# Moving eight key copies, two V casts and one normalisation within the fixed queues of a fused attention + MLP kernel

## The chip, the cores and the metric

The kernel runs on one core of a Trainium2 chip. A core has a matmul engine (TensorE, "PE" in the profile, with its weight loads shown as "PEld"), a vector engine (VectorE, "DVE"), an activation engine (ScalarE, "ACT"), GpSimd ("POOL") and a DMA-issuing engine (SyncE, "SP"). Each engine works through its own queue of instructions; engines wait for one another through semaphores. The metric is the device time of one execution in microseconds (us), the median of several runs. The profile is of one such execution; its span, 257.8 us, is a little shorter than the device time.

## The reference

Attention over 4 batches, 8 heads, 768 positions and head size 64, in which each query attends only to the 6 best of 24 key chunks of 32 positions (ranked by an upper bound on the score, causally masked), followed by an MLP with softplus.

```python
k_min, k_max = min / max of k over each chunk of 32 positions
ub     = sum over d of max(q*k_min, q*k_max)         # one bound per query and chunk
top    = the 6 chunks with the largest ub (causal)
scores = q @ k.T / sqrt(64), masked to the chosen chunks and to the causal triangle
attn   = exp(scores) / sum(exp(scores))
x      = attn @ v                                    # [3072 tokens, 512]
h      = x @ w_in                                    # [3072, 2048]
out    = softplus(h) @ w_out                         # [3072, 512]
```

## The kernel before

The 3072 tokens are cut into 12 blocks of 256 queries (batch b, block blk of three in the batch). Each block goes through the same steps. `prep`: transposed keys, their chunk minima and maxima, transposed queries, bounds, selection of chunks. `attend`: for each of 4 pairs of heads, scores, exponentials, product with V, normalisation, transposition to x. Then the MLP. The first three blocks (0, 1, 2, all of batch 0) are the ramp: they use TensorE transposes, and TensorE runs filler matmuls on zeros where it has nothing else to do, up to about 23 us. The nine others use DMA transposes, and their attention is mixed with the MLP of earlier blocks.

All instructions are made by small tasks. A scheduler in Python, which models durations, puts them in a fixed order on each engine; at the end, single tasks can be moved by hand. An entry (name, k, to, j) takes the k-th task called `name` that is still found in the order and puts it directly behind the j-th task called `to`. The last figure of a name is the block.

```python
for name, k, to, j in MOVES:
    t = [x for x in order if x.name == name][k]
    order.remove(t)
    order.insert(order.index([x for x in order if x.name == to][j]) + 1, t)
```

The parts of the ramp that matter here, with cuts marked. First the keys. Blocks 0 and 1 write their transposed keys whole into `ka_1`, a buffer that batch 1 needs later, and eight tasks `kcp` copy them to their places in `ka_0` and `kb_0`, which only block 2's scores read:

```python
# kT: PE transposes k -> ps;   kx: DVE, two tensor_reduce (max, min) per half of the heads
kr = add("DVE", 1.26, lambda: (red(0), red(1)), ..., name=f"kx{n}")            # L544
if split:                                          # blocks 0 and 1
    add("ACT", 0.5, kae, ..., name=f"ka{n}")                                   # L552: ka_1 <- ps
    for which, rs in (("ka", slice(0, 64)), ("kb", slice(64, 128))):
        add("DVE", 0.24, lambda: DV.tensor_copy(
            T(which, i)[rs, p2, ks_], T("ka", 1)[rs, p2, ks_]), ..., name=f"kcp{n}")   # L556
    continue
add("ACT", 1.06, lambda: (kab("ka", ...), kab("kb", ...)), ..., name=f"ka{n}")  # L541, block 2: ka_0, kb_0 <- ps
...
# kb0 (L371): DVE memset of 32 x 1536 words in kb_i;  ohka0, ohkb0 (L374): DVE copies of the one-hot rows
add("POOL", 0.6, lambda: PO.dma_start(*oh(which, i, blks)), ..., name="oh" + which)   # L377, for batch 1's ka_1, kb_1
```

Then the queries, the selection and V:

```python
# qT: PE transposes q -> ps;  qb: ACT evacuates it (L609);  qp, qn: DVE, positive and negative parts (L624)
# ub: PE, bounds from qp, qn and the chunk extremes (L646, L647)
# uba: DVE adds the causal mask (L653);  max: DVE MAX8 (L662);  lt: DVE, chunks below the sixth (L672, L675)
# mT: PE transposes the selection (L691);  ma: DVE or ACT evacuates it into qa (L696)
# vc: POOL or ACT casts V to bf16 (L721)
```

And a pair of heads in `attend`:

```python
# s:  PE scores (L749 keys, L756 selection; L775 from block 2 on);  ex: ACT exp (L785);  cm: POOL triangle (L791)
# av: PE product with V (L802)
add("DVE", 0.1, rc, ..., name=f"rc{n}")       # L811 reciprocal of the row sums, in ps
add("DVE", 0.34, nm, ..., name=f"nm{n}")      # L823 osb <- ps * st
add("PE", 0.12, tr, ..., name=f"oT{n}")       # L831 transposes osb -> ps
add("DVE", 0.22, xe, ..., name=f"xe{n}", alt=("ACT", ...))   # L836 x <- ps
# MLP: h: PE (L859), e and g: ACT exp and ln (L865, L869), y: PE (L885), yo: DVE (L890)
```

Of the kernel before, what the change touches and what calls it, by code (L numbers as in the profile page):

```python
# [54 lines left out]
HOLDS = [("q", 1, 1), ("q", 2, 1), ("q", 2, 1)]  # L55

READS = [("q", 1, 0), ("k", 2, 1)]
MOVES = [("holdp", 0, "vc0", 1), ("ldw_in", 0, "holdp", 0), ("ohka", 0, "vc2", 1), ("ohkb", 0, "ohka", 0)]
SHIFT = (0, 0, 8)


# [21 lines left out]
class Graph:  # L83
# [40 lines left out]
    def schedule(self):  # L124
# [157 lines left out]
        assert len(order) == len(self.tasks) + len(self.fills), (len(order), len(self.tasks))  # L282
        for name, k, to, j in MOVES:
            t = [x for x in order if x.name == name][k]
# [737 lines left out]
```

## Time and profile before

| | |
|---|---|
| device time, median of 3 | 259.45 us (259.43 to 259.63) |
| span of the profile | 257.8 us |
| DVE busy | 151.3 us (59%) |
| ACT busy | 199.1 us (77%) |
| POOL busy | 82.8 us (32%) |
| the eight copies, L556 | 285 to 514 ns each |
| memset of `kb`, L371 | 2 times 1338 ns |
| reductions kx of the ramp, L544 | 12 times, 681 ns each (median) |
| V casts on ACT, L721 | 0.65 us each at 15.97 and 16.97 us |

How to read it. The page lists each engine's busy time, the span in slices, and a chain of work followed back from the last instruction. A timeline line is "start, duration, engine, source line, operation, output <- input, count", and a bracket at its end gives how long the engine sat idle before it, and for whom it waited. A waits line is "engine line waited for: us in total, times, longest". A windows line gives the busy time of each engine in a stretch. A matmul's end is modelled, and consecutive matmuls overlap, so for TensorE the starts are what can be compared.

### The profile page before, as it was taken

The page shows a single profiled execution, that of the slowest core. Times are in us where ns is not written, and L with a number is a line of the kernel's source. Part 1 is how long each engine was busy: PE and PEld are TensorE (multiplying, and loading weights), DVE is VectorE, ACT ScalarE, POOL GpSimd, SP SyncE. Part 2 cuts the span into 40 slices and gives each one's busy share as a digit, 9 for nine tenths or more (in the row PEclk, how much of TensorE's full clock was granted, in tenths as well). Part 3 has the DMA queues.
Part 4 walks back from the last instruction along what each step waited for, and adds up shares of the span by engine and source line. Part 5 has one row for each costly group of instructions (what it writes and reads, how often), then busy time and mean ns, then how long its engine had stood idle before and what let it go on. Part 6 is the DMA issues. An engine that isn't in the chain of part 4 may idle for free.

```text
span 257.8 us, 6836 instructions
## 1 busy us (share of the span) xinstructions
PE 251.4 (98%) x2620; PEld 189.5 (73%) x2620; DVE 151.3 (59%) x555; ACT 199.1 (77%) x359; POOL 82.8 (32%) x176
## 2 busy tenths in 40 slices
PE   8999899999999999999999999999999999999994
PEld 6887696687685786878677778677677687686763
DVE  5897958459876983949797138586487310221101
ACT  2677989988494999899389979759689679796570
POOL 3352460356063460458223344323513001010000
PEclk9999999999999999999999999999999999999999
DMA  7999899999986979899963599654992310111202
GB/s 178 269 183 212 202 154 195 232 198 268 170 220 147 220 185 187 208 188 263 164 163 80 128 228 256 138 127 101 227 180 40 101 43 1 43 41 41 84 0 83
DMA packets 119897, 39.64 MB, mean 154 GB/s; under 512 B 113496, under 2 KB 115800, under 8 KB 119864
## 3 DMA queue, kind: packets, MB, share of 16 engines
q1 hardware_dynamic: 114456, 34.09, 60.5%
q0 software_dynamic: 3296, 4.59, 10.4%
q10 hardware_dynamic: 2112, 0.52, 0.9%
q8 instruction: 20, 0.33, 0.5%
q14 instruction: 13, 0.11, 0.1%
HBM read 27.26 MB, written 6.29 MB: 130 GB/s over the span
## 4 chain that ended last, share of the span: by engine, by line
PE 92%; DVE 6%; issue 1%; ACT 0%; DVEq 0%
PE ps L885 32%; PE ps L859 31%; PE ps L775 12%; PE ps L802 7%; PE ps L387 5%; PE ps L537 1%; PE ps L605 1%; DVE kx L571 1%; PE ps L647 1%; DVE qpn L624 1%; PE ps L831 1%; PE ps L646 1%; DVE yo L890 1%; DVE ka L556 1%; PE ps L749 1%; DVE kb L371 1%
## 5 line engine op out<-in xcount | busy, mean ns | idle before, releaser
L859 PE MATMUL ps<-x,w_in_sb 128*128 128x256 bf16 x768 | 100.9, 272 | 0.0
L785 ACT ACTIVATE pt<-ps 128x512 bf16<-128x512 f32 (+1 forms) x192 | 92.0, 562 | 7.8 <-PE ps L775 5.3
L885 PE MATMUL ps<-w_out_sb,g 128*128 128x512 bf16 (+1 forms) x400 | 97.2, 370 | 0.0
L859 PEld LDWEIGHTS <-w_in_sb 128*128 128x128 bf16 x768 | 72.0, 98 | 15.5 <-issue 0.7
L791 POOL TENSOR_SCALAR_AFFINE_SELECT pt<-pt 128x256 bf16<-128x256 bf16 x96 | 40.9, 433 | 126.7 <-ACT pt L785 126.6
L865 ACT ACTIVATE e<-ps 128x512 f32<-128x512 f32 x96 | 57.8, 617 | 30.3 <-PE ps L859 29.1
L885 PEld LDWEIGHTS <-g 128*128 128x128 bf16 x400 | 37.1, 98 | 25.0 <-ACT g L869 0.3
L869 ACT ACTIVATE g<-e 128x1024 bf16<-128x1024 f32 x48 | 51.5, 1072 | 1.0
L890 DVE COPY yo<-ps 128x512 f32<-128x512 f32 (+1 forms) x25 | 16.7, 667 | 44.2 <-PE ps L885 39.9
L811 DVE RECIPROCAL st<-ps 128x4 f32<-128x4 f32 x48 | 8.5, 178 | 36.9 <-PE ps L802 36.4
L802 PEld LDWEIGHTS <-pt 128*128 128x128 bf16 x672 | 26.5, 97 | 3.6
L802 PE MATMUL ps<-v,pt 128*128 128x65 bf16 x672 | 28.0, 193 | 0.0
L775 PE MATMUL ps<-qab,kb 128*128 128x256 bf16 (+1 forms) x168 | 25.8, 259 | 0.0
L775 PE MATMUL ps<-qab,ka 96*128 96x256 bf16 (+1 forms) x168 | 24.6, 259 | 0.0
L457 POOL CAST w<-w 128x512 bf16<-128x512 f32 x36 | 22.1, 628 | 5.2 <-DMA w<-in_q_dram 2.9
L571 DVE TENSOR_REDUCE kx<-w 128x32 bf16<-128x1024 bf16 x18 | 21.3, 1211 | 0.4 <-DMA w<-w 0.2
L775 PEld LDWEIGHTS <-ka 96*128 96x128 bf16 x168 | 15.4, 97 | 6.2 <-DVE qab L696 0.2
L775 PEld LDWEIGHTS <-kb 128*128 128x128 bf16 x168 | 14.7, 97 | 4.8
L387 PE MATMUL ps<-zero 128*128 128x256 bf16 x96 | 15.2, 294 | 1.1 <-DVE zero L355 1.1
L823 DVE TENSOR_TENSOR w<-ps,st 128x256 bf16<-128x256 f32 x36 | 15.2, 422 | 1.1
L662 DVE MAX8 ub<-ub 128x8 f32<-128x24 f32 (+2 forms) x160 | 14.2, 160 | 0.1
L455 POOL CAST v<-w 128x512 bf16<-128x512 f32 x18 | 11.0, 613 | 6.7 <-DMA w<-in_v_dram 6.7
(70 smaller groups left out, 181.9 us busy)
## 6 DMA issues: line engine op xcount, KB each, us to landing
w<-in_v_dram SPq DMA_DIRECT2D x24, 256.0 KB, 4.2
out_dram<-yo SPq DMA_DIRECT2D x23, 256.0 KB, 3.7
w<-in_k_dram SPq DMA_DIRECT2D x22, 256.0 KB, 4.0
w<-in_q_dram SPq DMA_DIRECT2D x22, 256.0 KB, 4.2
w_in_sb<-in_moe_w_in_dram POOLq DMA_DIRECT2D x2, 1024.0 KB, 11.6
w_out_sb<-in_moe_w_out_dram POOLq DMA_DIRECT2D x4, 512.0 KB, 8.9
w<-in_k_dram SPq DMA_DIRECT2D x2, 128.0 KB, 3.0
w<-in_k_dram ACTq DMA_DIRECT2D x2, 128.0 KB, 3.1
```

What stands on the lines that cost most here:

```text
L387: PE.matmul(T(Fill)[:, 0:256], T("zero")[:, 0:128], T("zero"), start=True, stop=True)
L457: PO.tensor_copy(T(b_)[:, :, t], T(xf).rearrange("s (p c) -> s p c", p=NP))
L571: DV.tensor_reduce(T(kx)[:, m].rearrange("d p (t c) -> d p t c", t=NT), T(kt).rearrange("d (p t) (c s) -> d p t c s", t=NT, s=CH), axis=AX ...
L775: PE.matmul(T(sp)[:, z * QB:z * QB + QB - q0], kk[r0:r1, p, (j + z) * 128:(j + z + 1) * 128], qq[r0:r1, p, q0:QB], start=True, stop=True)
L785: AC.activation(T(pt)[:, j:j + 2].rearrange("k j c -> k (j c)")[:, 0:w], T(sp)[:, 0:w], ACT.Exp, scale=SCALE)
L791: PO.affine_select(out=diag, in_=diag, compare_op=ALU.is_ge, fill=0.0, base=0, channel_multiplier=-1, pattern=[[0, 2], [1, 128]])
L802: PE.matmul(o[:, u, h], T(pts[h])[:, j, c0:c0 + 128], T("v", i)[:, j, 2 * p + h, :], start=(j == 0), stop=(j == t0 + u))
L859: PE.matmul(o, T("w_in")[:, dt, ft * 128:(ft + 1) * 128], T(x)[:, dt], start=(dt == 0), stop=(dt == KDM - 1))
L865: AC.activation(T(e)[:, f2 * 2:f2 * 2 + 2].rearrange("f a s -> f (a s)"), T(hp), ACT.Exp)
L869: AC.activation(T(gb)[:, f4 * 4:(f4 + 1) * 4], T(e), ACT.Ln, bias=1.0)
L885: PE.matmul(T(y)[:, 0:w], T(gb)[:, f, u * 128:(u + 1) * 128], T("w_out")[:, f, cs], start=(f == 0), stop=(f == KFF - 1))
L890: add("DVE", 0.06 + 0.54 / parts, lambda y=y, yo=yo, w=w: DV.tensor_copy(T(yo)[:, 0:w], T(y)[:, 0:w]), pr, r=[y], w=[yo], name=f"yo{n}")
```

## The change

The entries added to MOVES do three things.

- Key copies: all eight `kcp`, and batch 1's `kb0` memset ahead of them, go behind the last `xe1` on VectorE, that is behind the last piece of block 1's x. They stood between the one-hot copies and block 1's first normalisation; the memset stood a little behind that.
- V casts: the two ScalarE casts of block 1's V stood one between and one behind the evacuations of block 1's two query halves. Now both stand behind the second.
- Selection: block 1's second pair of `qp`, `qn` goes directly behind the first pair. The reciprocal and normalisation of block 0's last pair of heads (`rc0`, `nm0`, number 3), which stood ahead of the second half of block 1's selection, go behind it, and that pair's transposition (`oT0`) and evacuation (`xe0`) go back with them. The transposition and evacuation of the pair before it (number 2) move a few places too.

The aim is that work which something waits for does not stand behind work that nobody needs yet.

```diff
-MOVES = [("holdp", 0, "vc0", 1), ("ldw_in", 0, "holdp", 0), ("ohka", 0, "vc2", 1), ("ohkb", 0, "ohka", 0)]
+MOVES = [("holdp", 0, "vc0", 1), ("ldw_in", 0, "holdp", 0), ("ohka", 0, "vc2", 1), ("ohkb", 0, "ohka", 0),
+         ("kcp1", 0, "xe1", 3), ("kcp1", 0, "xe1", 3), ("kcp1", 0, "xe1", 3), ("kcp1", 0, "xe1", 3),
+         ("kcp0", 0, "xe1", 3), ("kcp0", 0, "xe1", 3), ("kcp0", 0, "xe1", 3), ("kcp0", 0, "xe1", 3),
+         ("kb0", 1, "xe1", 3), ("vc1", 0, "qb1", 1),
+         ("qp1", 1, "qn1", 0), ("qn1", 1, "qp1", 1),
+         ("oT0", 2, "av0", 7), ("xe0", 2, "oT0", 2),
+         ("rc0", 3, "lt1", 1), ("nm0", 3, "rc0", 3), ("oT0", 3, "mT1", 1), ("xe0", 3, "oT0", 3)]
```

(The lines are broken here for reading; in the file it is one line.) On VectorE the order from block 1's selection to block 2's keys is then:

```text
before: qp qn | uba max | qp qn | lt | rc0 nm0 | uba max lt | ma | kb0_0 ohka ohkb | 8 kcp | rc1 (bd) nm1 (v1) | kb0_1 | xe1 rc1 nm1 ... last xe1 | kx2 ...
after:  qp qn qp qn | uba max lt | uba max lt | rc0 nm0 | ma | kb0_0 ohka ohkb | rc1 (bd) nm1 (v1) | xe1 rc1 nm1 ... last xe1 | kb0_1 | 8 kcp | kx2 ...
```

GpSimd's and SyncE's orders are the same in both kernels.

More of the change, by code (lines that the diff above doesn't have):

```diff
@@ L57 @@
 READS = [("q", 1, 0), ("k", 2, 1)]
-MOVES = [("holdp", 0, "vc0", 1), ("ldw_in", 0, "holdp", 0), ("ohka", 0, "vc2", 1), ("ohkb", 0, "ohka", 0)]
+MOVES = [("holdp", 0, "vc0", 1), ("ldw_in", 0, "holdp", 0), ("ohka", 0, "vc2", 1), ("ohkb", 0, "ohka", 0), ("kcp1", 0, "xe1", 3), ("kcp1", 0, "xe1", 3), ("kcp1", 0, "xe1", 3), ("kcp1", 0, "xe1", 3), ("kcp0", 0, "xe1", 3), ("kcp0", 0, "xe1", 3), ("kcp0", 0, "xe1", 3), ("kcp0", 0, "xe1", 3), ("kb0", 1, "xe1", 3), ("vc1", 0, "qb1", 1), ("qp1", 1, "qn1", 0), ("qn1", 1, "qp1", 1), ("oT0", 2, "av0", 7), ("xe0", 2, "oT0", 2), ("rc0", 3, "lt1", 1), ("nm0", 3, "rc0", 3), ("oT0", 3, "mT1", 1), ("xe0", 3, "oT0", 3)]
 SHIFT = (0, 0, 8)
```

## The prediction

> **What bounds the kernel now.** I read the page first, then the waits, the chain of waits in order of time, the timelines of the ramp, and the windows. The page says who is full:
>
> ```profile
> PE 251.4 (98%) x2620; PEld 189.5 (73%) x2620; DVE 151.3 (59%) x555; ACT 199.1 (77%) x359; POOL 82.8 (32%) x176
> ```
>
> TensorE is missing only 257.8 - 251.4 = 6.4 us. The windows view puts 3.7 us of that into the tail after 250 us, 1.1 before the first matmul, and 0.7 in all between 45 and 250 us. So a delay or gain that reaches TensorE's queue by 45 us is handed on almost whole to the end. The one large gap left, with its cause in the same window:
>
> ```profile
> 25.00:30.00 5.00, 4.09 (x53) 2.56 (x49) 4.82 (x13) 4.97 (x11) 2.23 (x4) 1.00 0.81 179
> ```
>
> PE lacks 0.9 us, while DVE (4.82) and ACT (4.97) are full. The chain of waits shows what the gap waits for:
>
> ```profile
> 28.67 0.29 DVE ka L556
> 28.96 0.01 issue
> 28.97 0.29 DVE kb L556
> 29.26 0.03 issue
> 29.29 0.18 DVE st L811
> 29.48 0.22 DVE bd L369
> 29.69 0.02 issue
> 29.71 0.44 DVE osb L823
> 30.15 0.05 issue
> 30.20 0.28 PE ps L831 x2
> ```
>
> The reciprocal at 29.29 stands behind the eight key copies, though its product with V was issued on PE from 24.54 on and done by about 25.2. And the stage that the copies move to:
>
> ```profile
> 35.27 0.29 DVE L836 COPY x<-ps 128x256 bf16<-128x256 bf16 x1 [0.77 <-PE ps L831]
> 37.02 1.29 DVE L544 TENSOR_REDUCE kx<-ps 128x16 bf16<-128x512 f32 x2 [1.45 <-PE ps L537]
> 38.99 1.29 DVE L544 TENSOR_REDUCE kx<-ps 128x16 bf16<-128x512 f32 x2 [0.68 <-ACT kb L541]
> 40.31 0.36 DVE L588 COPY bd<-kx 64x64 bf16<-64x64 bf16 x2
> 40.79 0.98 DVE L624 TENSOR_SCALAR qpn<-qab 128x512 bf16<-128x512 bf16 x4
> ...
> 38.98 0.58 ACT L541 CAST ka<-ps 64x512 bf16<-64x512 f32 x1
> 39.57 0.58 ACT L541 CAST kb<-ps 64x512 bf16<-64x512 f32 x1
> 40.17 1.07 ACT L609 CAST qab<-ps 128x512 bf16<-128x512 f32 x2
> ```
>
> Between block 1's last x and block 2's reductions VectorE idles 1.45 us, and block 2's preparation is a chain in which DVE and ACT hand two PSUM tiles to each other.
>
> [...] the reciprocal just shown is 4 us late for no reason but its place. [...] the reduction at 38.99 waited 0.68 us for ACT's copy out of the same tile, which both only read. [...] six of the eight copies take 0.28 to 0.39 us, the two that met GpSimd's triangle masks at 27.70 took 0.51 and 0.40.
>
> **The change part by part.**
>
> V casts: in the trace the second query evacuation runs at 16.49, after a cast (0.65 us, start to next start 0.52), so it comes about 0.5 us earlier, at 16.0 or when its transposition (issued 15.55, 0.61) ends. The casts are needed for block 1's first product with V at 24.54 only.
>
> Selection: rc0 + nm0 take 19.33 to 19.88, 0.55 us, ahead of the second half of the selection; with them gone that half ends near 20.8 instead of 21.3. But TensorE does not get there sooner. Between 14.6 and block 1's first scores at 21.04 its queue holds 34 fillers x 0.109 = 3.7, two query transposes 0.9, and 1.6 of the rest = 6.2 of 6.4 us. The fillers keep their number, so at most 0.1 to 0.2 us is there. ACT gives it back: the last x evacuation of block 0 (0.38 us), which ran in idle time at 20.64, now falls after the first exponential. From 23.93 ACT runs without a gap to 32.3 us (exponentials 1.85 us per four). Before that it had idle stretches of 0.71 and 0.34 us, which take the evacuation up. Both parts: 0, plus or minus 0.1.
>
> Key copies, what they free: rc1 moves from 29.29 to about 26.4 (end of the one-hot copies), nm1 ends near 27.2, so the transposition starts when PE's queue reaches it, 28.48 + 4 x 0.109 = 28.92, not 30.20: 1.28 us. Then 8 matmuls (0.87) bring PE to 29.79 + 0.11 = 29.9, where the next product with V needs a PSUM tile whose exponential started at 29.50 and takes 0.56: 30.1. Before, this stood at 31.19. So 1.1 us stays. The following 8 matmuls stood at 32.13 behind a DVE copy delayed by the 1.34 us memset at 30.59, which moves too, but the masks end at 31.80 as before; I keep 1.1 to 1.2. The last transposition moves from 34.96 to 33.8, the last x copy from 35.27 to 34.1, and block 2's key transposes from 36.38 to 35.2.
>
> What they cost where they go: from the last x copy's end, 34.4, DVE runs the memset (1.34) to 35.75 and eight copies. GpSimd is idle there but for a V cast until 35.5, so I take the undisturbed spacing of the trace, 0.305 (26.82, 27.13, 27.43, 27.73): 8 x 0.305 = 2.44, ending at 38.2. Block 2's reductions start at 38.2, not 37.02. From here the chain, with the durations above:
>
> - first tile's reductions 38.2 to 39.5. ACT, done with the second tile at about 37.95 (its exponentials come 1.0 earlier, as its 0.9 us wait for osb at 32.3 falls away), waits for them 1.55 us;
> - ACT's two copies of that tile 39.53 to 40.7 (2 x 0.58 + 0.02), against 40.15 before; second tile's reductions 39.5 to 40.8;
> - query evacuations 40.72 to 41.8 (1.07), against 41.24 before;
> - qp, qn second pair: 41.83 to 42.3, against 41.77 before;
> - bounds on PE end at about 42.55, when the last of the two inputs is there and 7 x 0.026 follow.
>
> TensorE: from block 2's key transposes at 35.2 it has 1.74 (transposes) + 20 x 0.109 + 4 x 0.216 = 4.8 us, to 40.0, then wants the tile that ACT leaves at 40.7: 0.75 us of wait. Another 0.86 brings it to 41.6, where the bounds wait about 0.7 for qn. Afterwards it stands at 42.55. Before, the matmuls after the bounds began at 42.45.
>
> Sum at that point: -1.15 (gap) + 0.75 + 0.7 = +0.3 by the waits, +0.1 by the positions; I take the positions, which do not add roundings. The selection, its transposition (45.48 before, its input ready at about 44.85) and the later MLP groups then shift along: the exponentials that hold their tiles end over 2 us before their use. The w_out pieces that the next matmuls need landed 1.8 to 2.7 us before their first use, and the queue that loads them is untouched.
>
> **The rivals.** (1) The gap is closed and nothing takes its place: -1.1 us, 258.3. It needs block 2's reductions no later than PE's new arrival; for it speaks DVE's 1.45 us of idle time, against it that 3.8 us of work go into them and that both tiles and ACT stand behind. (2) The copies are slower than undisturbed (the eight took 2.84 us where they stood): +0.4 more, 260.0. (3) Other waits of PE later on swallow a small shift: bounds waited 0.35 us at 89.8 and 0.20 at 106.2 for qpn; for it that their chains hang partly on DMA; it would pull any result towards 0. (4) The earlier selection and queries start block 1's scores earlier by 0.5: 258.9 or so; against it the fillers and ACT's unbroken run.
>
> **Range and chances.** 259.45 + 0.1 = 259.55; rival 2 is a little likelier than 1, so 259.6. The gain and the two waits are each known to some 0.2 us, so 0.35 together, and rivals 1 and 2 bound the rest: 258.7 to 260.1. 2% is 5.2 us, more than four times the largest part of any of it, so 0.98 for within 2%, and 0.01 for each side.
>
> **What would show it.** Right: no idle time of PE before L831 near 29; the last x copy near 34.1; eight L556 copies about 0.3 us apart up to 38.2; an ACT wait of about 1.5 us for L544 before its L541 copies; PE waits of together about 1.4 us between 40 and 42.6, one for ACT kb and one for DVE qpn. Wrong: the reductions start by 37.3, or PE reaches the bounds near 41 without a wait (rival 1), or PE still waits near 29, or the first exponential of block 1 starts well before 21.7 (rival 4).

## The result and the profile after

| | before | after |
|---|---|---|
| device time, median of 4 runs | 259.54 us (259.43 to 259.83) | 260.47 us (260.41 to 260.61) |
| ratio, 95% | | 1.0035 [1.0018, 1.0052] |
| device time in a second session | 259.81 us (75 runs) | 260.46 us (22 runs) |
| ratio there, 95% | | 1.0030 [1.0014, 1.0046] |
| span of the profile | 257.8 us | 258.7 us |

The change makes the kernel slower by about 0.3%, or 0.4 to 1.2 us by the second interval. The prediction had 259.6 us, with a loss of 0.1 us by its sum, and a range that ended at 260.1. First the lines that answer to those shown of before. The page of after, busy time per engine:

```profile
PE 252.7 (98%) x2620; PEld 189.8 (73%) x2620; DVE 150.0 (58%) x555; ACT 199.1 (77%) x359; POOL 83.1 (32%) x176
```

The windows view of after, where the columns are the busy time of PE, PEld, DVE, ACT and POOL, the granted clock, the DMA share and GB/s:

```profile
25.00:30.00 5.00, 5.00 (x73) 3.55 (x68) 3.12 (x7) 4.97 (x12) 2.52 (x5) 1.00 0.90 201
40.00:45.00 5.00, 4.29 (x38) 2.45 (x36) 4.70 (x22) 4.23 (x8) 0.98 (x2) 1.00 1.13 181
```

The 0.9 us gap of TensorE between 25 and 30 us is closed, and VectorE has room there (3.12 of 5.00, where it had 4.82). A gap of 0.7 has opened between 40 and 45. The stage that the copies moved to, in the timeline of VectorE of after:

```profile
35.16 0.29 DVE L836 COPY x<-ps 128x256 bf16<-128x256 bf16 x1 [0.77 <-PE ps L831]
35.70 1.34 DVE L371 MEMSET kb<- 32x1536 uint32 x1 [0.26 <-issue]
37.05 0.29 DVE L556 COPY kb<-ka 64x512 bf16<-64x512 bf16 x1
...
39.19 0.28 DVE L556 COPY ka<-ka 64x512 bf16<-64x512 bf16 x1
39.40 2.47 DVE L544 TENSOR_REDUCE kx<-ps 128x16 bf16<-128x512 f32 x4
41.90 0.36 DVE L588 COPY bd<-kx 64x64 bf16<-64x64 bf16 x2
42.52 0.49 DVE L624 TENSOR_SCALAR qpn<-qab 128x512 bf16<-128x512 bf16 x2 [0.25 <-ACT qab L609]
```

the timeline of ScalarE of after:

```profile
40.70 0.58 ACT L541 CAST ka<-ps 64x512 bf16<-64x512 f32 x1 [1.82 <-DVE kx L544]
41.29 0.58 ACT L541 CAST kb<-ps 64x512 bf16<-64x512 f32 x1
41.90 1.07 ACT L609 CAST qab<-ps 128x512 bf16<-128x512 f32 x2
```

and the timeline of TensorE of after:

```profile
40.19 1.03 PE L885 MATMUL ps<-w_out_sb,g 128*128 128x512 bf16 x4
41.92 1.02 PE L885 MATMUL ps<-w_out_sb,g 128*128 128x512 bf16 x4 [0.70 <-ACT kb L541]
42.87 0.20 PE L646 MATMUL ps<-bd,qpn 128*128 128x48 bf16 x1
...
43.75 0.92 PE L859 MATMUL ps<-x,w_in_sb 128*128 128x256 bf16 x7
```

So the shape that was predicted is there: memset, eight copies 0.3 us apart, ScalarE waiting 1.82 us for the reductions, TensorE waiting for ScalarE's tile and then for qn. All of it stands about 1.2 us later than predicted, of which 1.04 us (0.67 + 0.37 in the sum below) had arisen before TensorE came to the old gap at all.

**Where the 0.92 us of span comes from.** Matmuls are counted off in both traces, and the start of the k-th one of a line compared. The differences, in us, of two profiles of after (the one shown, and "again" from the second session) and of a second profile of the unchanged kernel, each against the first profile of before:

| matmul (start in before) | after | after again | before again |
|---|---|---|---|
| first query transposes, block 0 (6.67) | +0.58 | +0.44 | +0.41 |
| query transposes, block 1 (14.82) | +0.67 | +1.01 | +0.81 |
| scores, second pair of heads of block 1 (23.22) | +1.04 | +1.39 | +0.81 |
| key transposes, block 2 (36.38) | -0.12 | +0.22 | +0.81 |
| first after block 2's bounds (42.45) | +1.30 | +1.65 | +0.81 |
| L859 number 129 (66.54) | +1.03 | +1.62 | +1.13 |
| L859 number 257 (103.47) | +0.91 | +1.50 | +1.01 |
| end of span (257.82) | +0.92 | +2.51 | +1.0 |

The column "after" is a sum that closes: +0.67 in the start-up, +0.37 within block 1's first scores, -1.16 in the old gap, +1.42 in the new waits, -0.27 and -0.12 later. Three of these terms need a word, and the experiments are about them: the 0.67 is not the change's, the 0.37 was not foreseen, and the rest of the copies' account comes out at +0.26.

**The start-up.** These are lines of TensorE's timeline, of before:

```profile
5.80 1.04 PE L387 MATMUL ps<-zero 128*128 128x256 bf16 x8
6.67 0.60 PE L605 MATMUL ps<-identf,w 128*128 128x128 f32 x4
```

of after:

```profile
5.80 1.62 PE L387 MATMUL ps<-zero 128*128 128x256 bf16 x8
7.25 0.60 PE L605 MATMUL ps<-identf,w 128*128 128x128 f32 x4
```

and of before again, the same kernel as the first:

```profile
5.80 1.45 PE L387 MATMUL ps<-zero 128*128 128x256 bf16 x8
7.08 0.60 PE L605 MATMUL ps<-identf,w 128*128 128x128 f32 x4
```

The same eight fillers start at the same 5.80 and take 1.04, 1.62 or 1.45 us: none, five or four of them run at half pace (starts 0.21 us apart, then 0.109). What sets the moment of the change is not shown: the granted clock reads 1.00 in each microsecond up to 10 us, in before and in after. The moment itself differs widely: full pace begins at 3.87 us in e2, 5.80 in before and 7.03 in after, and over thirteen profiles of eleven kernels the first query transposes start between 6.02 and 7.25 us. In before again the shift lasted to the end (+0.81 becomes +1.0). A profile of either kernel is thus worth only what remains when its start is subtracted; from here on "net" means counted from block 1's query transposes.

**The wait that was not foreseen.** The timeline of TensorE of before at block 1's first scores:

```profile
21.04 0.39 PE L749 MATMUL ps<-qab,ka 64*128 64x256 bf16 x4
...
21.48 0.33 PE L749 MATMUL ps<-qab,ka 64*128 64x256 bf16 x4
```

the timeline of VectorE of before, with block 0's last reciprocal and normalisation:

```profile
19.33 0.17 DVE L811 RECIPROCAL st<-ps 128x4 f32<-128x4 f32 x1
19.54 0.42 DVE L823 TENSOR_TENSOR osb<-ps,st 128x256 bf16<-128x256 f32 x1
```

the timeline of TensorE of after at the same scores:

```profile
21.59 0.39 PE L749 MATMUL ps<-qab,ka 64*128 64x256 bf16 x4
21.82 0.38 PE L756 MATMUL ps<-qab,ohb 64*128 64x256 bf16 x4
22.04 0.65 PE L749 MATMUL ps<-qab,ka 64*128 64x256 bf16 x3
...
22.53 0.21 PE L749 MATMUL ps<-qab,ka 64*128 64x128 bf16 x1
```

and the chain of waits of after (start, length, what):

```profile
21.74 0.09 DVE mr L675
21.83 0.09 DVE st L811
21.92 0.02 issue
21.94 0.43 DVE osb L823
22.38 0.04 issue
22.42 0.23 PE ps L749
```

The second group of scores (22.04) follows the first by 0.45 us as in before, but stretches to 0.65 where it took 0.33. The chain says what it stretches for: it writes the PSUM tile of block 0's last product with V, and that tile is read by exactly the reciprocal and the normalisation which the change puts behind the selection. They were at 19.33 to 19.96 in before; now they end at 22.36. The list of waits does not show it: the stretched duration and the chain are the only signs. The first group came 0.12 us earlier net, since pair 3's transposition no longer stands ahead of it, and that transposition takes the same 0.11 back behind the selection; so the 0.37 is the wait alone.

### The profile page after: what moved, and what is told of

Same layout as the page of the kernel before. It is cut to its first block, busy times and chain, and to the rows that moved or that the text cites. A ratio compares the mean times of both kernels' runs of the same rounds, so it can differ in the third digit from the quotient of the medians.

```text
span 258.7 us, 6834 instructions
## 1 busy us (share of the span) xinstructions
PE 252.7 (98%) x2620; PEld 189.8 (73%) x2620; DVE 150.0 (58%) x555; ACT 199.1 (77%) x359; POOL 83.1 (32%) x176
## 4 chain that ended last, share of the span: by engine, by line
PE 89%; DVE 5%; ACT 3%; issue 1%; ACTq 0%; DVEq 0%
PE ps L885 32%; PE ps L859 29%; PE ps L775 12%; PE ps L802 7%; PE ps L387 4%; ACT pt L785 2%; PE ps L647 1%; PE ps L537 1%; DVE kx L571 1%; PE ps L646 1%; DVE qpn L624 1%; PE ps L605 1%; DVE yo L890 1%; PE ps L831 1%; DVE kb L371 1%
## 5 line engine op out<-in xcount | busy, mean ns | idle before, releaser
L859 PE MATMUL ps<-x,w_in_sb 128*128 128x256 bf16 x768 | 100.9, 273 | 0.0
L859 PEld LDWEIGHTS <-w_in_sb 128*128 128x128 bf16 x768 | 71.9, 98 | 15.5 <-issue 0.7
```

The source lines that it names most:

```text
L859: PE.matmul(o, T("w_in")[:, dt, ft * 128:(ft + 1) * 128], T(x)[:, dt], start=(dt == 0), stop=(dt == KDM - 1))
```

## The experiments

Each list below is appended to the four entries that MOVES has in before. KC are the key copies and the memset behind the last `xe1`; VC the V cast; QP the earlier second `qp`, `qn`; O2 the moved transposition of pair 2; RC the group around `rc0`, `nm0` number 3. KC + VC + QP + O2 + RC is the change. Ratios are to before, run on the same chip; a session had 43 to 75 runs of before, with medians of 259.81 to 259.97 us, and 14 to 22 of each version. A ratio need not be the quotient of the medians (e11's medians would give 1.0025, its ratio is 1.0006).

**One half each.**

```diff
+ e1: KC                      # key copies and memset only
+ e2: VC + QP + O2 + RC       # everything else
```

> Only the key copies and the memset move behind the last x of block 1; V casts and selection stay as before. Theory A (the key copies lose in block 2's preparation what they free near 29 us; the selection part costs 0.4 us more, because block 1's second score group must wait for the PSUM tile of block 0's last normalisation): no wait of TensorE near 22 us, transposition L831 near 28.9 instead of 30.2, last x copy near 34.2, block 2's reductions near 38.4, two waits of TensorE between 40 and 43, and the matmuls behind the bounds 0.3 to 0.5 us later than before; total +0.1 to +0.5 us against before. Theory B (the selection part alone makes the change slower, the copies gain): total -0.6 us or better. [...]

> Only V casts and selection move; the key copies stay. Theory A: block 1's second score group waits for the normalisation moved behind the selection, about 0.4 us, which goes on through the VectorE queue to the transposition near 30: total +0.2 to +0.5 us. Theory B: the whole +0.9 us. Theory of the change's author, that the earlier selection helps: -0.2 us or better.

Measured: e1 260.3 us, 1.0005 [0.9987, 1.0024]; e2 260.26 us, 1.0013 [0.9998, 1.0028]. Neither half differs for certain from before by its time. The profiles tell more. e1, net: no change up to block 1's scores, -1.16 at block 2's key transposes, +0.27 after the bounds, +0.14 at the end. e2, net: +0.37 at block 1's scores, with the same stretched group of 0.64 us, and +0.20 from the old gap on, which was still there and swallowed the rest. So the gap, its closing and its return belong to the copies; the stretched group belongs to the other half.

**The copies spread out.** If the memset and eight copies in a row make block 2's reductions late, they should be put where VectorE idles.

```diff
+ SP = [("kcp1",0,"nm1",3)]*2 + [("kcp1",0,"xe1",0)]*2 + [("kcp0",0,"xe1",0)]*2
+    + [("kcp0",0,"v1",1)]*2 + [("kb0",1,"v1",1)]
+ e3: SP + VC + QP + O2 + RC
+ e4: SP
```

> The whole change, but the memset and the eight copies stand in idle stretches of VectorE's queue: memset and two copies behind block 1's first normalisation, four behind its first x, two behind its last normalisation. Theory A: the transposition near 29 and nothing behind it is late, block 2's reductions start when their transposes end, and the waits between 40 and 43 are gone: about 0.8 us faster than before (1.2 gained, 0.4 lost by the selection part), 1.7 us faster than the changed kernel. Theory B (place of the copies does not matter): like the changed kernel, +0.9 us.

> As the one before, without V casts and selection moved. Theory A: the full gap is gained, 1.1 to 1.2 us faster than before, 0.4 us faster than with the selection part. Theory that the selection part is worth something once the copies are out of the way: slower than the one before.

Measured: e3 260.38 us, 1.0019 [1.0003, 1.0035]; e4 259.97 us, 1.0007 [0.9984, 1.003]. e4 does what was wanted up to 42 us: the waits before the bounds are gone and the lead over before is 1.15 us net. It still gains nothing. Of the lead, 0.6 is lost at 51 us, of which 0.3 comes back at 63; between 66 and 86 all of it is lost and more, and the end is +0.38 net. The first loss is a product with V that waits for a GpSimd mask, which stands in GpSimd's queue behind a cast that waits for block 3's keys. The second is in the timeline of VectorE of e4:

```profile
68.78 2.35 DVE L571 TENSOR_REDUCE kx<-w 128x32 bf16<-128x1024 bf16 x2 [3.03 <-DMA w<-w]
```

In before that reduction ran at 65.95 without a wait. Its input is a DMA transpose issued at 62.39 (61.53 in before). So TensorE came early, and its data did not. e3 is not easily read in the profile (one `bd` copy took 1.37 us instead of 0.38 and delayed it by 0.46 before block 1's scores), but the stretched group of 0.64 us is in it as in all runs with RC.

**Repeats.** After and before, unchanged, in one session.

> The changed kernel itself once more, with more executions, beside its like before. Theory A ([...] the rest is the lost wait on block 0's last normalisation and block 2's preparation): the difference against before shrinks to +0.4 to +0.7 us in the median, and single executions of both kernels scatter over more than 1 us. Theory C (the slow start belongs to the changed kernel): +0.9 us again, and its profile shows the first query transposes at 7.2 us again, not near 6.0 to 6.7.

> The kernel before, unchanged, as a run of its own: a null comparison and a second profile of it. Theory A: ratio 1 within its interval; its first query transposes start anywhere between 6.0 and 7.3 us, and what differs at 7 us is found again at the end, unless a later wait takes it up. Theory C: first query transposes at 6.67 us again, to 0.1 us.

Measured: after 260.46 us, 1.0030 [1.0014, 1.0046]; before 260.08 us, 1.0007 [0.9991, 1.0023]. The loss is there again, and the unchanged kernel differs from itself by nothing that its interval can tell from 1. Single executions of one kernel spread over 259 to 262 us there, which is why a single profile cannot settle a few tenths. The profile of after again has the 0.37 us once more, and at the end another +1.0 between 104 and 125 us, where two bounds waited for qpn; that is one execution, and the first profile of after does not have it.

**Are the loads held too long?** Block 3's key loads wait for a piece of w_out to land. Both kernels get a hold on an earlier piece.

```diff
- LGATE = hold_sp(*prev[-2], pr)          # waits for piece 2
+ LGATE = hold_sp(*prev[-2], pr, at=1)    # waits for piece 1
+ e7: SP and this;  e8: before and this
```

> Copies spread over idle stretches of VectorE (as in the run with the copies spread alone), and in addition the small DMA that holds back block 3's loads waits for the second piece of w_out instead of the third; the order of instructions is the same. Theory D (behind TensorE's queue stands a second chain, from the w_out transfers over the held-back loads of block 3 to GpSimd's casts and the DMA transposes, and it takes the gain of the spread copies away at 51 and at 66 to 75 us): block 3's loads start about 2.5 us earlier, the waits at 51 and near 72 vanish, and the kernel is 0.6 to 1.2 us faster than before. Rival (the loads are not what is late): no faster than the spread copies alone, 0 to +0.2 us against before.

> The kernel before with the held-back loads of block 3 let go at the second piece of w_out, nothing else. Theory D: here TensorE's own queue is late and the loads are not waited for, so 0 to -0.3 us. Rival (the loads are late in the kernel before too): -0.5 us or better; second rival: loads that start earlier slow the last w_out piece, and TensorE waits for it near 49 us: +0.3 us or more.

Measured: e7 260.53 us, 1.0019 [1.0, 1.0039]; e8 260.06 us, 1.0011 [0.9992, 1.003]. No gain: this idea failed. In e7 the loads were issued at 40.89 instead of 43.88, and landed only at 49.5, 8.6 us later, and the reduction behind block 4's transpose again waited 2.99 us. The DMA share is 1.15 between 40 and 45 us in e7, and the earlier issue did not bring an earlier landing: counted from its own start-up, e7's loads landed within 0.2 us of e4's, which were issued at 44.78. The profile of e8 was late by 1.03 us before its gate could matter, because a load of V came late: ScalarE's cast waited for it until 21.12 (the later V cast of before ran at 16.97), and behind the cast stood the copy for which TensorE then waited 0.85 us. Such landings are a part of the spread of single executions.

**The change without its normalisation part.**

```diff
+ e9: KC + VC + QP + O2       # rc0, nm0 number 3 stay where they were
```

> The whole change, but rc0 and nm0 number 3 stay ahead of the second half of block 1's selection, with their transposition and evacuation. Missed-wait theory: block 1's second group of scores (L749) writes the PSUM tile that rc0 and nm0 read, and waits for them only where they come later; here its 0.37 us wait is gone, the gap between the selection's second transposition (L691) and that group is as before within 0.05 us, and the time falls from after's 1.003 to about 1.0015 of before (260.1 us where before has 259.8). Rival, the two parts do not add (the later waits for ACT's kb and for qn swallow the 0.37, since they are set by DVE's chain): the wait is gone, the wait at the bounds grows by as much, and the time stays at 1.003.

Measured: 259.78 us where before has 259.97, 0.9987 [0.9964, 1.0009]. Its interval lies wholly below that of after again, 1.0030 [1.0014, 1.0046]. The timeline of TensorE of e9:

```profile
21.39 0.39 PE L749 MATMUL ps<-qab,ka 64*128 64x256 bf16 x4
...
21.84 0.33 PE L749 MATMUL ps<-qab,ka 64*128 64x256 bf16 x4
```

The second group is back at 0.33 us, and net 0.01 from before. After the bounds e9 is at +0.27 net, as e1 is, and after at +0.63: the two parts add there, and the rival, by which the waits at the bounds would swallow the 0.37, is out. At the end the profiles of e9 and after both stand at about +0.25 net, so the difference of their times is not in these two executions; it rests on the timed runs, and on the profile of after again. The timed runs give the sign and not the size: the ratios differ by 0.0043, which is 1.1 us, where the wait is 0.37 us, they come from two chips, and 1.0015 was expected for e9. Nor do they show the +0.27 of the copies, since neither e1 nor e9 is slower than before for certain.

**Where a lead goes.** Two more kernels with the lead, and with one cast on GpSimd taken out of the way.

```diff
+ e10: SP + [("ck3", 0, "cm2", 1)]            # cast of block 3's keys behind block 2's second mask
+ e11: KC without the memset + the same cast
```

> The spread copies alone, and on GpSimd the first cast of block 3's keys behind block 2's second triangle mask instead of ahead of it. Absorption theory: the wait of block 2's product with V for that mask (0.37 us at 51.5, as the mask stood behind the cast, which stood behind its load) is gone, and the matmuls at 52 us keep the lead of about 1.1 us over before that they had at 42.45, each counted from block 1's query transposes; but the DMA transposes behind block 4's keys still take the lead between 66 and 86 us, so that the time is 0.999 to 1.001 of before. Rival, the mask was the only thing in the way: the lead holds to the end, 1.1 us, ratio 0.996.

> The key copies of the change without the memset of kb (it stays where it was), and the cast moved as in the run before. The eight copies then end near 34.4 + 2.44 + 0.25 = 37.1 us, where block 2's reductions began in before. Theory (memset plus copies make the late chain): ACT's wait for the reductions falls from 1.8 us to under 0.5, TensorE's two waits before the bounds from 1.25 to under 0.3 together, and the matmuls after the bounds lead before by 0.9 to 1.1 us, counted from block 1's query transposes; the end then shows whether a lead lasts: 0.999 to 1.001 if the DMA transposes between 66 and 86 us take it, 0.996 to 0.997 if not. Rival, the copies alone already make the chain late (TensorE comes 1.2 us earlier and meets the same tiles): the waits are still 0.8 us or more and the lead at the bounds is under 0.3.

Measured: e10 260.63 us, 1.0021 [1.0003, 1.0038]; e11 260.61 us, 1.0006 [0.9982, 1.003]. e10 is slower than before, and not within the 0.999 to 1.001 expected. Its wait for the mask is gone and the lead at 52 us is 1.0 us net, as expected. Then it is lost, and 1.1 us more, earlier than expected, between 52 and 66: a reduction of block 3 now waits for its transpose. The timeline of VectorE of e10:

```profile
58.74 2.35 DVE L571 TENSOR_REDUCE kx<-w 128x32 bf16<-128x1024 bf16 x2 [1.91 <-DMA w<-w]
```

e11 kept a lead, but a small one: 0.40 us after the bounds (0.9 to 1.1 expected) and 0.57 at the end of its profile, within what its timed runs can't tell from nothing. ScalarE's wait was 1.15 us, not under 0.5, and TensorE's two waits came to 0.76, not under 0.3. The timeline of VectorE of e11 shows the reason,

```profile
34.55 1.21 DVE L556 COPY kb<-ka 64x512 bf16<-64x512 bf16 x1
35.77 0.29 DVE L556 COPY ka<-ka 64x512 bf16<-64x512 bf16 x1
```

and the timeline of GpSimd of e11:

```profile
34.95 0.65 POOL L721 CAST v<-w 128x512 bf16<-128x512 f32 x1
```

The first copy ran beside GpSimd's V cast and took 1.21 us, 0.9 longer than the others. What held it is not shown: the delay is longer than the cast's 0.65 us, and the copy's record begins 0.40 us before the cast's.

**What sets the pace of the loads.** GpSimd issues the w_out loads behind its masks, and the masks wait for ScalarE's exponentials of block 1. The same two lines of the timelines of GpSimd and of SyncE's queue, of before (with the last mask ahead of them):

```profile
31.39 0.41 POOL L791 TENSOR_SCALAR_AFFINE_SELECT pt<-pt 128x256 bf16<-128x256 bf16 x1 [0.46 <-ACT pt L785]
...
31.87 2.98 POOL L469 DMA_DIRECT2D w_out_sb<-in_moe_w_out_dram  x4
...
43.88 1.02 SPq L447 DMA_DIRECT2D w<-in_k_dram  x2
```

of after:

```profile
32.91 2.99 POOL L469 DMA_DIRECT2D w_out_sb<-in_moe_w_out_dram  x4
...
45.07 1.03 SPq L447 DMA_DIRECT2D w<-in_k_dram  x2
```

and of e4:

```profile
32.48 2.99 POOL L469 DMA_DIRECT2D w_out_sb<-in_moe_w_out_dram  x4
...
44.78 1.05 SPq L447 DMA_DIRECT2D w<-in_k_dram  x2
```

In all thirteen profiles the w_out loads come 8.20 us after the scores of block 1's second pair of heads (their second group, 23.67 in before), and in the eleven without the earlier hold the key loads come 11.65 to 12.49 us after that. It makes no difference to the w_out loads whether TensorE won a microsecond at 29 us or not. The missed 0.37 us, on the other hand, is handed to them in full: it lies ahead of those scores.

## Why the prediction was wrong

**The failed step is "Both parts: 0, plus or minus 0.1".** The V casts and the earlier qp and qn did cost nothing that shows. The selection cost 0.36 to 0.38 us in the four profiles with RC (in e3 with the 0.46 us of the `bd` copy taken off), and 0.00 to 0.01 in those of before again, e1, e4 and e9. The prediction counted what TensorE's queue holds up to block 1's first scores, found no gain, and looked for a loss only on ScalarE. It did not ask which PSUM tile the scores write and who reads it last. The answer was the very pair of instructions that was being moved back. Its term should have been +0.37: the second group wants the tile from 22.04 on, and the normalisation ends at 22.36, which lets the waiting matmul go at 22.42. The expected gain did not come either. The second half of the selection started its MAX8 at 20.70 in after, 0.17 us earlier net than in before, not 0.5, since VectorE then waited 0.33 us for TensorE's bounds.

**The key copies: mechanism right, sizes nearly.** The gap closed by 1.16 us net (1.1 to 1.2 predicted). e1, the profile with the least shift of its start, has the copies' stage as it was computed: first wait 0.87 at the MLP's product (0.75 predicted), second 0.55 at the bounds (0.7), net +0.27 behind them. The prediction had +0.3 by its waits and +0.1 by its positions, and chose the positions; that the sum of the waits came so close is luck in part, as each of them was off by 0.12 to 0.15, in opposite directions. What the positions left out is the 0.26 us between a copy's end and the memset's start, charged to "issue" in the profile of after; the profile of before has it too, in front of its first such memset at 23.02. About half of it was made up, since the reductions began before the last copy had ended: they started at 38.33 in e1, where 38.2 was predicted.

**"A delay or gain that reaches TensorE's queue by 45 us is handed on almost whole to the end" fails for gains.** It was read from TensorE having only 0.7 us of idle time between 45 and 250 us. That it is hardly ever idle at the pace of before does not say that its inputs would be there sooner. The profiles of e4, e7 and e10 led by about 1.15 us and ended with no lead, as VectorE waited up to 3 us for transposes of block 3's and 4's keys, whose loads keep a time of their own. A smaller lead did last, the 0.40 us of e11. For delays it held in part: after's +0.63 net behind the bounds was +0.25 at the end of one profile, and in the other +0.64 was still +0.49 at 103 us. Hence rival 1 (gap closed, nothing in its place: -1.1) would not have come true even where its condition was met, as e4 shows. Rival 3 was right in kind. Rival 2 was not met: the copies took 0.30 us each. Rival 4 fell: the first scores came 0.12 us earlier net, not 0.5. Two readings were slightly off and bear on nothing: the tail after 250 us holds 3.5 us of TensorE's idle time and not 3.7, since the window ran past the span's end, and the first of the eight copies (0.39 us) also ran beside a GpSimd mask.

**The sum as it should have been:** 0.37 (the tile) + 0.27 (copies, memset, issue) = 0.64 us, which is the +0.63 net found after the bounds in the profile and lies within the 0.4 to 1.2 us of the timed runs. About 260.1 would have been the prediction. It is not shown that this sum reaches the end as it stands: the two profiles of after end at +0.25 and +1.50 net. The rest of the first session's 0.93 us is not settled. The profile's start-up shift of 0.67 accounts for it in that one execution, but there is no trace of the other three.

No version was shown to beat before. e9 beats after (0.9987 against 1.0030, each to before on its own chip) and is the form of the change in which no loss was measured.

## What to carry to other kernels

Before moving a reader of a PSUM tile back, look up the next writer of that tile: a postponed normalisation can become a wait for whichever matmul gets the tile next, even where nobody needs its result yet (0.37 us in after). A closed gap on the busiest engine is worth only as much as its inputs can follow (e4 led by 1.15 us and ended with no lead); find what starts the loads (here, ScalarE's exponentials through GpSimd's queue) and ask whether the change moves that. And subtract the start-up before two traces are compared: the same kernel differed from itself by 0.8 us there.

## What was not expected of the hardware

- The moment at which TensorE goes to full pace differed by 3.2 us between executions (3.87 us in e2, 7.03 in after; first query transposes at 6.02 and 7.25). In before again the 0.81 us of its start-up were still there at the end of a 258 us kernel.
- A DMA transpose of block 4's keys that landed within 4.4 us in before took 6.3 us in e4, issued 0.9 us later among other loads; loads issued 3 us earlier, at a DMA share of 1.15, landed no earlier (e7).
- A VectorE copy that takes 0.29 us elsewhere in e11 took 1.21 there beside a GpSimd cast of 0.65 us, which is a delay longer than the whole cast.
- A 32 x 1536 memset on VectorE starts 0.26 us after the copy ahead of it (at 35.70 in after, at 23.02 in before), where the eight copies behind it in after start 0.02 us after one another's end.
